# First dense layer of a fused attention and MLP kernel: two 128x512 tiles in two neighbouring PSUM banks, one tanh and one product for both

## The chip, the cores and the metric

The kernel runs on one core of one Trainium2 chip. The metric is the device time of one execution in microseconds; the time before is the median of three runs. Line numbers (L623) are those of the kernel before, as the profile uses them. Engines: PE is TensorE, ACT ScalarE, DVE VectorE, POOL GpSimd, SP the engine that issues most DMAs.

## The reference

```python
def _A_ref(x, wq, wk, wv, wo):              # 32 heads of 16, one shared key and value head
    q = (x @ wq).reshape(B, S, H, Dh).transpose(0, 2, 1, 3)
    k = x @ wk
    v = x @ wv
    p = softmax(einsum("bhqd,bkd->bhqk", q, k) * Dh ** -0.5)
    o = einsum("bhqk,bkd->bhqd", p, v)
    return o.transpose(0, 2, 1, 3).reshape(B, S, H * Dh) @ wo

def _B_ref(x, w1, w2):
    return einsum("bsf,fd->bsd", silu(einsum("bsd,df->bsf", x, w1)), w2)

xn = layernorm(x)                            # x: 1 x 2048 x 512, F = 1792, all bf16
return x + _A_ref(xn, wq, wk, wv, wo) * silu(_B_ref(xn, w1, w2))
```

## The kernel before

**What is computed in which tiles.** Queries come in 4 chunks of 512 (c), heads in 8 groups of 4 (g), so there are 32 groups (gi); keys come in 16 tiles of 128 (kt). For one group and one key tile there are four score blocks of 128 keys x 512 queries, one per head; they use four row quarters of the TensorE array. 32 x 16 x 4 = 2048 blocks have to be exponentiated. A *tile* of attention is the four blocks of one group and key tile, and the planner gives each tile to one of two engines:

- ScalarE: two blocks go into the two banks of psA0 or psA1 (`fill_A`), and one ACTIVATE of 1024 columns exponentiates both into `pa_sb` (`exp_A`, L623).
- VectorE: each block goes into a single bank out of D, D1 (the two halves of psD) and F (psF) (`fill_D`), and one TENSOR_SCALAR (`exp_D`, L661) turns it into an int16 whose bits are a rough exponential. Two blocks in D and D1 may go in one instruction of 1024 columns. When all four blocks of a tile are done, POOL makes two shifted copies (`shift`, L686), and the three together weigh out the error.

The products with the values (`emit_PV`, L745) run in four column quarters into psO, one group of four matmuls for a ScalarE block of each head, three for a VectorE block.

**Dense work.** The first layer of the MLP is the jobs `("h", c, ft)`: 4 chunks x 14 tiles of 128 rows of F, each of 4 groups of 4 column matmuls ("slots") into bank F. Silu is made as (tanh(z/2) + 1) * z: when the matmuls are done ScalarE makes a tanh of the bank into `t_sb` (`emit_tanh`, L1061), and VectorE multiplies it with the bank into `u_sb` (`evac`, L1093). The factors of a half are taken up later. The second layer is the jobs `("z", tt)`, 16 of 14 slots each, with the same tanh and product into `tmp_sb`. Jobs `q` (queries of a chunk, 4 slots), `w` and `wp` (output projection, 4 and 3 slots) use bank F as well, and end with one VectorE instruction.

PSUM has eight banks here: psA0 and psA1 two each, psD two, psO one, psF one.

**What sets the order.** The order of every engine's instructions is written out ahead by a planner in the kernel's Python: it keeps a clock per engine with its own costs, and semaphores are put where the order needs them. Its loop goes round once for each ScalarE exponential: it takes some slots of other TensorE work (a dense job if the dense work is behind its plan, else PV), and then `score_run` puts one burst of score matmuls: the two ScalarE blocks, and in the same burst, on the other row quarters, VectorE blocks for the banks that are free (`fill_D`). A burst may start when psA is free again (`release`) and is wanted 0.685 us before ScalarE's end (`needed`); a bank that becomes free up to SLIP = 0.2 us after the burst's start is still taken. `fill_D` is called from the burst alone while ScalarE has tiles left. A tanh is put in front of the next exponential when its bank is ready (`tanh_ready`). `hold` says whether a bank has a VectorE block ("blk") or a dense job ("job"); bank F goes to a dense job if one is due. VectorE's instructions are taken as they become ready (`advance_v`).

How many tiles go to VectorE isn't fixed: `next_D` opens another tile whenever a free bank asks for a block, and ScalarE goes on with what is left.

The lines that carry this in `score_run` are

```python
            fill_A(tile, rows, state["n"] % 2)
            fill_D(t, other(rows))
            if tanh_ready(K.act_end - TGATE):
                emit_tanh()
            exp_A(tile[0], [(i, tile[1], None, 512 * m) for m, i in enumerate(rows)])
```

Of the kernel before, what the change touches and what calls it, by code (L numbers as in the profile page):

```python
# [5 lines left out]
ACT = mybir.ActivationFunctionType  # L6
# [7 lines left out]
P = 128  # L14
# [201 lines left out]
def bass_recurrent_scan__grouped_kv_mqa__dense_activation_silu__prompt_kernel(  # L216
# [24 lines left out]
    NPA = 11  # L241
    DEFER, PATIENCE = .2,8
    NPD = 4
    NPS = 3
    NGN = 2
    NOB = 4
# [26 lines left out]
    with ExitStack() as es:  # L273
        def sb(name, shape, dt=BF16):
            return es.enter_context(nc.sbuf_tensor(name, shape, dt))
# [114 lines left out]
        def stats_act(t):  # L390

            r = D ** -0.5
            op("a", lambda e: e.activation(scr_sb[:, 1:2], eps_sb[:, 0:1], ACT.Sqrt), reads=["eps"], writes=["scr1"], cost=4)
            op("a", lambda e: e.activation(t_sb[:, 0, :], x_sb[:, t, :], ACT.Copy, scale=1.0 / D, accum_out=mv_sb[:, t, 0:1]),
               reads=[("x", t)], writes=[("t", 0), ("mean", t)], cost=NQ)
            op("a", lambda e: e.activation(nm_sb[:, 0:1], mv_sb[:, t, 0:1], ACT.Copy, scale=r), reads=[("mean", t)],
               writes=["nm"], cost=4)
            op("a", lambda e: e.activation(t_sb[:, 1, :], x_sb[:, t, :], ACT.Square, scale=-r, bias=nm_sb[:, 0:1],
                                           accum_out=mv_sb[:, t, 1:2]),
               reads=[("x", t), "nm"], writes=[("t", 1), ("mv", t)], cost=NQ)  # L400

# [470 lines left out]

        dense = [("h", 0, ft) for ft in range(NFT)]
        for c in range(1, NC):
            for ft in range(NFT):
                dense.append(("h", c, ft))
                if ft in (2, 6, 9, 13):
                    dense.append(("z", 4 * (c - 1) + (2, 6, 9, 13).index(ft)))  # L880
# [96 lines left out]
        def next_job(t):  # L977
# [3 lines left out]
                return None  # L981
            return next((jb for jb in jobs[:AHEAD] if startable(jb, t)), None)

        def job_ready(t):
            if jst["open"]:
                return True
            return bool(jobs and "F" in free_banks(t + 0.04) and next_job(t))

        def emit_job(t, n):
            if not jst["open"]:  # L990
                jb = next_job(t)
                jobs.remove(jb)
                b = "F"
                jst.update(open=jb, part=0, bank=b)
                hold[b] = "job"
            jb, b = jst["open"], jst["bank"]
            k, ap = jb[0], bank_ap(b)
            items = list(range(jst["part"], min(SIZE[k], jst["part"] + n)))
            end = SIZE[k] - 1
            if k in ("h", "q"):  # L1000
                _, c, ft = jb
                w, name = (w1_sb, "w1") if k == "h" else (wq_sb, "wq")
                rd = xnT_keys(c) + [name]

                def pair(m):
                    return w[:, m, ft * P:(ft + 1) * P], xnT_sb[:, m, c * NQ:(c + 1) * NQ]
# [19 lines left out]
            op("pe", f, reads=rd, writes=[b], cost=("col", [0, 1, 2, 3] * len(items), NQ))  # L1026
            jst["part"] += len(items)
            if k != "wp":
                jst["slots"] += len(items)
            if jst["part"] == SIZE[k]:  # L1030
                jst["open"] = None
                if k in ("h", "z"):
                    jst["tanh"].append((jb, b))
                else:
                    task(k, evac, 0.69, jb=jb, bank=b, reads=[b], writes=[])
                if k in ("z", "w"):
                    tok.add((k + "mm", jb[1]))
            return len(items)
# [13 lines left out]

        def tanh_ready(t):
            return jst["tanh"] and (state["nt"] < 2 or ("tev", state["nt"] - 2) in tok) and \
                K.ready("a", [jst["tanh"][0][1]], [("t", state["nt"] % 2)]) <= t

        def emit_tanh():
            jb, b = jst["tanh"].pop(0)
            n = state["nt"]
            state["nt"] += 1  # L1060
            op("a", lambda e: e.activation(t_sb[:, n % 2, :], bank_ap(b), ACT.Tanh, scale=0.5 if jb[0] == "h" else 0.25),  # L1061
               reads=[b], writes=[("t", n % 2)], cost=NQ)
            task(jb[0], evac, 0.685, jb=jb, bank=b, n=n, reads=[b, ("t", n % 2)], writes=[])

        def load_xr(tt):
            if tt < NT:
# [10 lines left out]

        def add(tk):
            tt = tk["jb"][1]
            final_add("v", tt, fin_sb[:, tt % 2, :], ("fin", tt % 2))  # L1080
            tok.add(("add", tt))

        def evac(tk):
            k, jb, b = tk["kind"], tk["jb"], tk["bank"]
            src = bank_ap(b)
            hold[b] = None
            if k in ("h", "z"):
                n = tk["n"]
                if k == "h":
                    dst, key = u_sb[:, jb[1] % 2, jb[2], :], ("u", jb[1] % 2, jb[2])  # L1090
                else:
                    dst, key = tmp_sb[:, (jb[1] // 4) % 2, jb[1] % 4, :], ("tmp", jb[1] % 8)
                op("v", lambda e: e.scalar_tensor_tensor(out=dst, in0=t_sb[:, n % 2, :], scalar=1.0, in1=src,  # L1093
                                                         op0=ALU.add, op1=ALU.mult),
                   reads=tk["reads"], writes=[key], cost=tk["cost"])
                tok.add(("tev", n))
                tok.add((k + "ev",) + jb[1:])
            elif k == "q":
                _, c, t = jb
                op("v", lambda e: e.tensor_scalar(qT_sb[:, c % 2, t, :], src, QSCALE, None, op0=ALU.mult),  # L1100
# [1 line left out]
                tok.add(jb)  # L1102
            elif k == "w":
                tt = jb[1]
                op("v", lambda e: e.scalar_tensor_tensor(out=fin_sb[:, tt % 2, :], in0=src, scalar=0.25,
                                                         in1=tmp_sb[:, (tt // 4) % 2, tt % 4, :],
                                                         op0=ALU.mult, op1=ALU.mult),
                   reads=[b, ("tmp", tt % 8)], writes=[("fin", tt % 2)], cost=tk["cost"])
                tok.add(("wev", tt))
                task("add", add, 0.42, jb=jb, reads=[("fin", tt % 2), ("x", 12 + tt % 4)], writes=[])  # L1110
# [165 lines left out]
        def extra_fill():  # L1276
# [6 lines left out]
            ride = max(needed(), t + 0.2) + 0.43  # L1283
            best = None
            for b in BANKS:
                if hold[b] is None and (b != "F" or not jobs or not behind(F_BEHIND) or not next_job(t)):
# [221 lines left out]
```

## Time and profile before

| | |
|---|---|
| Median of three runs | 676.16 us (676.15 to 676.19) |
| Profiled execution | 676.35 us, of which the span of the trace is 674.5 |
| Mean granted TensorE clock | 0.998 |
| ScalarE busy | 666.4 us (99%), 769 instructions: 677 exponentials, 72 tanhs and a few others |
| TensorE busy | 651.8 us (97%) |
| VectorE busy | 586.9 us (87%), 986 instructions |
| POOL busy | 364.3 us (54%), 371 instructions |
| First-layer tiles | 56 tanhs and 56 products of 128x512 |

Busy time is the union of the instructions' durations. Instructions of an engine overlap in this profile (one starts before the last has ended), so the spacing of two starts or ends, and not the duration, is what an instruction costs an engine that is always busy. The number behind a bar in the rows of groups is the engine's idle time just ahead of the group, with what ended it.

### The profile page before, as it was taken

What the parts mean: (1) busy time and instruction counts of PE and PEld (TensorE: products, weight loads), DVE (VectorE), ACT (ScalarE), POOL (GpSimd) and SP (SyncE); (2) the same over time, 40 slices, a digit from 0 to 9 for tenths busy, and PEclk for the clock granted to TensorE, in tenths of its full rate; (3) what the DMA queues carried; (4) which work ended last, traced back from release to release, by engine and by line L of the source; (5) the groups of instructions that cost most, each with busy time, mean ns of one, the idle gap of its engine ahead of it and who ended that gap; (6) DMA issues with size and microseconds to landing.
All of it is one profiled execution on the core that took longest, in us unless ns stands there. A gap on an engine that the chain in (4) does not pass through costs nothing.

```text
span 674.5 us, 18636 instructions
## 1 busy us (share of the span) xinstructions
PE 651.8 (97%) x8175; PEld 184.7 (27%) x8182; DVE 586.9 (87%) x986; ACT 666.4 (99%) x769; POOL 364.3 (54%) x371
## 2 busy tenths in 40 slices
PE   8999999999999999999999999999999999999997
PEld 4422222222222222222222222222222222222221
DVE  7998889889899888988898988888898788878996
ACT  8999999999999999999999999999999999999997
POOL 3255555556556555555555655464565466645662
PEclk9999999999999999999999999999999999999999
DMA  6440000000000000000000000010000000000110
GB/s 167 148 143 2 1 2 1 2 2 1 2 2 1 17 17 18 18 1 2 2 1 3 2 1 2 2 32 29 6 2 2 1 2 2 1 2 2 32 34 32
DMA packets 12321, 12.50 MB, mean 19 GB/s; under 512 B 2512, under 2 KB 11728, under 8 KB 12240
## 3 DMA queue, kind: packets, MB, share of 16 engines
q1 hardware_dynamic: 11680, 10.78, 5.2%
q8 instruction: 64, 1.05, 0.7%
q10 hardware_dynamic: 560, 0.52, 0.2%
q14 instruction: 17, 0.14, 0.1%
HBM read 8.95 MB, written 2.10 MB: 16 GB/s over the span
## 4 chain that ended last, share of the span: by engine, by line
ACT 87%; PE 9%; DVE 2%; DMA 1%; SPq 1%; issue 0%
ACT pa_sb L623 82%; ACT t_sb L1061 5%; PE psA L593 3%; PE psO L745 3%; PE psF L372 2%; DMA x_sb<-in_A_x_dram 1%; PE psD L432 0%; PE psD L463 0%; DVE stats_sb L388 0%; DMA kTb_sb<-kTa_sb 0%; SPq L481 0%; DVE kTa_sb L475 0%; PE psA L639 0%; PE psD L593 0%; DVE wq_sb L1441 0%
## 5 line engine op out<-in xcount | busy, mean ns | idle before, releaser
L623 ACT ACTIVATE pa_sb<-psA 128x1024 bf16<-128x1024 f32 x677 | 642.7, 1202 | 0.9 <-PE psA L593 0.6
L686 POOL INT64_ADD ph_sb<-ph_sb x286 | 294.2, 1041 | 224.0 <-DVE ph_sb L661 224.0
L661 DVE TENSOR_SCALAR ph_sb<-psD 128x512 int16<-128x512 f32 (+1 forms) x501 | 343.2, 698 | 47.2 <-PE psD L593 39.2
L745 PE MATMUL psO<-ph_sb,vaug_sb 128*32 128x512 bf16 x1716 | 216.2, 383 | 0.2
L745 PE MATMUL psO<-pa_sb,vaug_sb 128*32 128x512 bf16 x1362 | 204.7, 383 | 0.3 <-ACT pa_sb L623 0.3
L593 PE MATMUL psA<-qT_sb,kTa_sb 32*128 32x512 bf16 x692 | 134.2, 384 | 7.9 <-ACT pa_sb L623 6.3
L593 PE MATMUL psA<-qT_sb,kTb_sb 32*128 32x512 bf16 x654 | 126.8, 384 | 7.5 <-ACT pa_sb L623 6.7
L593 PE MATMUL psD<-qT_sb,kTb_sb 32*128 32x512 bf16 x328 | 117.7, 384 | 0.2 <-DMA kTb_sb<-kTa_sb 0.2
L593 PE MATMUL psD<-qT_sb,kTa_sb 32*128 32x512 bf16 x301 | 106.8, 384 | 0.0
L661 DVE TENSOR_SCALAR x_sb<-psD 128x512 int16<-128x512 f32 (+1 forms) x111 | 76.3, 694 | 15.6 <-PE psD L593 14.5
L686 POOL INT64_ADD x_sb<-x_sb x60 | 61.7, 1041 | 51.5 <-DVE x_sb L661 51.5
L593 PEld LDWEIGHTS psA<-qT_sb,kTa_sb 32*128 32x128 bf16 x692 | 32.5, 90 | 147.2 <-ACT pa_sb L623 135.1
L593 PEld LDWEIGHTS psA<-qT_sb,kTb_sb 32*128 32x128 bf16 x654 | 30.7, 91 | 143.6 <-ACT pa_sb L623 134.7
L372 PE MATMUL psF<-xnT_sb,w_sb 128*32 128x512 bf16 x896 | 69.5, 384 | 0.0
L372 PE MATMUL psF<-w_sb,u_sb 128*32 128x512 bf16 x896 | 69.0, 384 | 0.0
L745 PE MATMUL psO<-x_sb,vaug_sb 128*32 128x512 bf16 x366 | 68.0, 384 | 0.0
L745 PEld LDWEIGHTS psO<-ph_sb,vaug_sb 128*32 128x32 bf16 x1716 | 53.2, 94 | 48.0 <-issue 31.2
L745 PEld LDWEIGHTS psO<-pa_sb,vaug_sb 128*32 128x32 bf16 x1362 | 50.7, 94 | 46.6 <-issue 33.6
L1061 ACT ACTIVATE t_sb<-psF 128x512 bf16<-128x512 f32 x72 | 55.7, 774 | 0.0
L1093 DVE SCALAR_TENSOR_TENSOR u_sb<-t_sb,psF 128x512 bf16<-128x512 bf16 x56 | 38.2, 683 | 11.0 <-ACT t_sb L1061 8.8
L661 DVE TENSOR_SCALAR ph_sb<-psF 128x512 int16<-128x512 f32 x56 | 38.1, 680 | 0.0
L593 PEld LDWEIGHTS psD<-qT_sb,kTb_sb 32*128 32x128 bf16 x328 | 28.1, 91 | 0.6 <-DMA kTb_sb<-kTa_sb 0.5
(131 smaller groups left out, 362.1 us busy)
## 6 DMA issues: line engine op xcount, KB each, us to landing
w_sb<-in_B_w_dram SPq DMA_DIRECT2D x2, 1792.0 KB, 8.6
x_sb<-in_A_x_dram SPq DMA_DIRECT2D x18, 128.0 KB, 2.3
out_dram<-ob_sb SPq DMA_DIRECT2D x14, 128.0 KB, 1.7
x_sb<-in_A_x_dram SPq DMA_DIRECT2D x3, 512.0 KB, 5.7
wop_sb<-in_A_wo_dram SPq DMA_DIRECT2D x1, 512.0 KB, 4.0
wq_sb<-in_A_wq_dram SPq DMA_DIRECT2D x1, 384.0 KB, 6.5
x_sb<-in_A_x_dram ACTq DMA_DIRECT2D x2, 128.0 KB, 2.9
kTb_sb<-kTa_sb SPq DMA_DIRECT2D x16, 16.0 KB, 2.6
```

Source lines behind the costliest of these rows:

```text
L372: r = e.matmul(bank[32 * i:32 * i + 32, :], lhsT=lhsT[:, 32 * i:32 * i + 32], rhs=rhs, start=start, stop=stop, tile_position=(0, 32 * i), ...
L593: return e.matmul(ap, lhsT=kT_sb[g % 2][32 * i:32 * i + 32, kt * P:(kt + 1) * P], rhs=qT_sb[32 * i:32 * i + 32, c % 2, g // 2, :], start=T ...
L623: d = op("a", lambda e: e.activation(pa_sb[:, sl, :], psA[k][:, :], ACT.Exp, scale=ESCALE), reads=["A%d" % k], writes=[("pa", sl)], cost=2 ...
L661: d = op("v", lambda e: e.tensor_scalar(ph_ap(0, sl, 512 * pos, 512 * pos + m), src, float(PH_ONE + PH_BIAS), 0.0, op0=ALU.add, op1=ALU.ma ...
L686: d = op("gp", lambda e, j=j: e.int64_add(ph_ap(j, sl, 0, 4 * NQ).bitcast(I64), ph_ap(0, sl, 0, 4 * NQ).bitcast(I64), PH_SHIFT[j] * 0x0001 ...
L745: r = e.matmul(psO[32 * i:32 * i + 32, cs], lhsT=vaug_sb[:, p["v"], p["kt"], :], rhs=p["ap"], start=s0, stop=s1, tile_position=(0, 32 * i) ...
L1061: op("a", lambda e: e.activation(t_sb[:, n % 2, :], bank_ap(b), ACT.Tanh, scale=0.5 if jb[0] == "h" else 0.25), reads=[b], writes=[("t", n ...
L1093: op("v", lambda e: e.scalar_tensor_tensor(out=dst, in0=t_sb[:, n % 2, :], scalar=1.0, in1=src, op0=ALU.add, op1=ALU.mult), reads=tk["read ...
```

## The change

First-layer jobs come in pairs: `("h", c, ft)` with even ft stands for the tiles ft and ft + 1, and has 8 slots. Slots 0 to 3 go into bank F with the weights of tile ft + 1, slots 4 to 7 into bank D1 with those of tile ft. So that both can be read in one access, psD grows to 1536 columns and psF becomes its last 512: D, D1 and F are neighbours. One tanh of 1024 columns reads D1 and F, and one product of 1024 columns writes both tiles of `u_sb`; `t_sb` has two rows of 1024. The second-layer jobs, q, w and wp stay in bank F alone, with a tanh of 512 columns.

Bank D1 is taken by the job when its second half starts, and only when it is free (`job_ready`, `emit_job`); from slot 4 on, `fill_D` keeps D1 from VectorE blocks for it. Both banks are given back when the product is put into VectorE's order. Second-layer jobs stand behind the first-layer tiles 2, 6, 8 and 12 instead of 2, 6, 9 and 13. `fin_sb` goes: the gated product of the last layer is written to `ob_sb`, and the residual is added in place.

```diff
-        t_sb = sb("t_sb", [P, 2, NQ])
+        t_sb = sb("t_sb", [P, 2, 2, NQ])
-        fin_sb = sb("fin_sb", [P, 2, D])
...
-        psD = es.enter_context(nc.psum_tensor("psD", [P, 1024], FP32))
+        psD = es.enter_context(nc.psum_tensor("psD", [P, 1536], FP32))
-        psF = es.enter_context(nc.psum_tensor("psF", [P, 512], FP32))
+        psF = psD[:, 1024:1536]
...
-        dense = [("h", 0, ft) for ft in range(NFT)]
+        dense = [("h", 0, ft) for ft in range(0, NFT, 2)]
...
-        SIZE = dict(h=4, z=NFT, q=4, w=4, wp=3)
+        SIZE = dict(h=8, z=NFT, q=4, w=4, wp=3)
...
         def job_ready(t):
             if jst["open"]:
-                return True
+                return jst["open"][0] != "h" or jst["part"] < 4 or hold["D1"] == "job" or "D1" in free_banks(t + 0.04)
...
         def emit_job(t, n):
...
+            if k == "h" and jst["part"] + n > 4 and hold["D1"] != "job":
+                if "D1" in free_banks(t + 0.04 + 0.21 * max(0, 4 - jst["part"])):
+                    hold["D1"] = "job"
+                else:
+                    n = 4 - jst["part"]
...
                 for m in items:
                     l, r = pair(m)
-                    h = columns(e, ap, l, r, m == 0, m == end)
+                    if k == "h":
+                        h = columns(e, bank_ap(("F", "D1")[m // 4]), l, r, m % 4 == 0, m % 4 == 3)
+                    else:
+                        h = columns(e, ap, l, r, m == 0, m == end)
...
         def emit_tanh():
...
-            op("a", lambda e: e.activation(t_sb[:, n % 2, :], bank_ap(b), ACT.Tanh, scale=0.5 if jb[0] == "h" else 0.25),
-               reads=[b], writes=[("t", n % 2)], cost=NQ)
+            if jb[0] == "h":
+                op("a", lambda e: e.activation(t_sb[:, n % 2, :, :].rearrange("p a n -> p (a n)"), psD[:, NQ:3 * NQ], ACT.Tanh, scale=0.5),
+                   reads=bs, writes=[("t", n % 2)], cost=2 * NQ)
+            else:
+                op("a", lambda e: e.activation(t_sb[:, n % 2, 0, :], psF[:, :], ACT.Tanh, scale=0.25),
+                   reads=bs, writes=[("t", n % 2)], cost=NQ)
...
         def evac(tk):
...
                 if k == "h":
-                    dst, key = u_sb[:, jb[1] % 2, jb[2], :], ("u", jb[1] % 2, jb[2])
+                    _, c, ft = jb
+                    dst, keys = u_sb[:, c % 2, ft:ft + 2, :], [("u", c % 2, ft), ("u", c % 2, ft + 1)]
+                    dst, tin = dst.rearrange("p a n -> p (a n)"), t_sb[:, n % 2, :, :].rearrange("p a n -> p (a n)")
+                    src2 = psD[:, NQ:3 * NQ]
...
-                op("v", lambda e: e.scalar_tensor_tensor(out=fin_sb[:, tt % 2, :], in0=src, scalar=0.25,
+                op("v", lambda e: e.scalar_tensor_tensor(out=ob_sb[:, tt % NOB, :], in0=src, scalar=0.25,
...
         def fill_D(t, free, only=None):
 
-            banks = sorted(free_banks(t + SLIP), key=lambda b: (b == "F", K.ready("pe", [], [b])))
+            jb = next_job(t) if jobs and behind(F_BEHIND) else None
+            want = ["F"]
+            if jst["open"] and jst["open"][0] == "h" and jst["part"] >= D1_PART and hold["D1"] != "job":
+                want = ["D1"]
+            banks = sorted(free_banks(t + SLIP), key=lambda b: (b in want, b == "F", K.ready("pe", [], [b])))
             if only:
                 banks = only
             keep = 0
-            if not only and "F" in banks and jobs and behind(F_BEHIND) and next_job(t):
-                keep = 1
+            if not only and (want == ["D1"] or jb and not jst["open"]):
+                keep = len(set(banks) & set(want))
```

More of the change, by code (lines that the diff above doesn't have):

```diff
@@ L243, in bass_recurrent_scan__grouped_kv_mqa__dense_activation_silu__prompt_kernel @@
     NPD = 4
+    D1_PART = 4
     NPS = 3
@@ L393, in stats_act @@
             op("a", lambda e: e.activation(scr_sb[:, 1:2], eps_sb[:, 0:1], ACT.Sqrt), reads=["eps"], writes=["scr1"], cost=4)
-            op("a", lambda e: e.activation(t_sb[:, 0, :], x_sb[:, t, :], ACT.Copy, scale=1.0 / D, accum_out=mv_sb[:, t, 0:1]),
+            op("a", lambda e: e.activation(t_sb[:, 0, 0, :], x_sb[:, t, :], ACT.Copy, scale=1.0 / D, accum_out=mv_sb[:, t, 0:1]),
                reads=[("x", t)], writes=[("t", 0), ("mean", t)], cost=NQ)
@@ L397, in stats_act @@
                writes=["nm"], cost=4)
-            op("a", lambda e: e.activation(t_sb[:, 1, :], x_sb[:, t, :], ACT.Square, scale=-r, bias=nm_sb[:, 0:1],
+            op("a", lambda e: e.activation(t_sb[:, 1, 0, :], x_sb[:, t, :], ACT.Square, scale=-r, bias=nm_sb[:, 0:1],
                                            accum_out=mv_sb[:, t, 1:2]),
@@ L871, in partial @@
                reads=["ident", ("spart", k)], writes=[key, *more], cost=("full", [None], NQ))
-        dense = [("h", 0, ft) for ft in range(NFT)]
+        dense = [("h", 0, ft) for ft in range(0, NFT, 2)]
         for c in range(1, NC):
-            for ft in range(NFT):
+            for ft in range(0, NFT, 2):
                 dense.append(("h", c, ft))
-                if ft in (2, 6, 9, 13):
-                    dense.append(("z", 4 * (c - 1) + (2, 6, 9, 13).index(ft)))
+                if ft in (2, 6, 8, 12):
+                    dense.append(("z", 4 * (c - 1) + (2, 6, 8, 12).index(ft)))
         dense += [("z", tt) for tt in range(4 * (NC - 1), 4 * NC)]
-        SIZE = dict(h=4, z=NFT, q=4, w=4, wp=3)
+        SIZE = dict(h=8, z=NFT, q=4, w=4, wp=3)
         total = sum(SIZE[jb[0]] for jb in dense) + 28 * SIZE["q"]
@@ L982, in next_job, with job_banks @@
             return next((jb for jb in jobs[:AHEAD] if startable(jb, t)), None)
+        def job_banks(jb):
+            return ["D1", "F"] if jb[0] == "h" else ["F"]
         def job_ready(t):
             if jst["open"]:
-                return True
+                return jst["open"][0] != "h" or jst["part"] < 4 or hold["D1"] == "job" or "D1" in free_banks(t + 0.04)
             return bool(jobs and "F" in free_banks(t + 0.04) and next_job(t))
@@ L992, in emit_job @@
                 jobs.remove(jb)
[L993 to L996, printed above, removed]
+                jst.update(open=jb, part=0)
+                hold["F"] = "job"
+            jb, b = jst["open"], "F"
             k, ap = jb[0], bank_ap(b)
+            if k == "h" and jst["part"] + n > 4 and hold["D1"] != "job":
[3 more added lines that the diff above has]
+                    n = 4 - jst["part"]
+            wr = [b]
             items = list(range(jst["part"], min(SIZE[k], jst["part"] + n)))
@@ L1005, in pair @@
                 def pair(m):
-                    return w[:, m, ft * P:(ft + 1) * P], xnT_sb[:, m, c * NQ:(c + 1) * NQ]
+                    f, m = (ft + 1 - m // 4 if k == "h" else ft), m % 4
+                    return w[:, m, f * P:(f + 1) * P], xnT_sb[:, m, c * NQ:(c + 1) * NQ]
+                if k == "h":
+                    wr = sorted({"FD"[m // 4] + "1" * (m // 4) for m in items})
             elif k == "z":
@@ L1023, in f @@
                     l, r = pair(m)
-                    h = columns(e, ap, l, r, m == 0, m == end)
+                    if k == "h":
+                        h = columns(e, bank_ap(("F", "D1")[m // 4]), l, r, m % 4 == 0, m % 4 == 3)
+                    else:
+                        h = columns(e, ap, l, r, m == 0, m == end)
                 return h
-            op("pe", f, reads=rd, writes=[b], cost=("col", [0, 1, 2, 3] * len(items), NQ))
+            op("pe", f, reads=rd, writes=wr, cost=("col", [0, 1, 2, 3] * len(items), NQ))
             jst["part"] += len(items)
@@ L1032, in emit_job @@
                 if k in ("h", "z"):
-                    jst["tanh"].append((jb, b))
+                    jst["tanh"].append((jb, job_banks(jb)))
                 else:
-                    task(k, evac, 0.69, jb=jb, bank=b, reads=[b], writes=[])
+                    task(k, evac, 0.69, jb=jb, bank=b, reads=[b], writes=[("ob", jb[1] % NOB)] if k == "w" else [])
                 if k in ("z", "w"):
@@ L1054, in tanh_ready @@
             return jst["tanh"] and (state["nt"] < 2 or ("tev", state["nt"] - 2) in tok) and \
-                K.ready("a", [jst["tanh"][0][1]], [("t", state["nt"] % 2)]) <= t
+                K.ready("a", jst["tanh"][0][1], [("t", state["nt"] % 2)]) <= t
         def emit_tanh():
-            jb, b = jst["tanh"].pop(0)
+            jb, bs = jst["tanh"].pop(0)
             n = state["nt"]
             state["nt"] += 1
-            op("a", lambda e: e.activation(t_sb[:, n % 2, :], bank_ap(b), ACT.Tanh, scale=0.5 if jb[0] == "h" else 0.25),
-               reads=[b], writes=[("t", n % 2)], cost=NQ)
-            task(jb[0], evac, 0.685, jb=jb, bank=b, n=n, reads=[b, ("t", n % 2)], writes=[])
+            if jb[0] == "h":
[4 more added lines that the diff above has]
+                   reads=bs, writes=[("t", n % 2)], cost=NQ)
+            task(jb[0], evac, 1.219 if jb[0] == "h" else 0.685, jb=jb, bank=bs, n=n, reads=bs + [("t", n % 2)], writes=[])
         def load_xr(tt):
@@ L1079, in add @@
             tt = tk["jb"][1]
-            final_add("v", tt, fin_sb[:, tt % 2, :], ("fin", tt % 2))
+            final_add("v", tt, ob_sb[:, tt % NOB, :], ("ob", tt % NOB))
             tok.add(("add", tt))
@@ L1084, in evac @@
             k, jb, b = tk["kind"], tk["jb"], tk["bank"]
-            src = bank_ap(b)
-            hold[b] = None
+            bs = b if isinstance(b, list) else [b]
+            src = bank_ap(bs[-1])
+            for b1 in bs:
+                hold[b1] = None
             if k in ("h", "z"):
                 n = tk["n"]
+                tin, src2 = t_sb[:, n % 2, 0, :], src
                 if k == "h":
-                    dst, key = u_sb[:, jb[1] % 2, jb[2], :], ("u", jb[1] % 2, jb[2])
-                else:
-                    dst, key = tmp_sb[:, (jb[1] // 4) % 2, jb[1] % 4, :], ("tmp", jb[1] % 8)
-                op("v", lambda e: e.scalar_tensor_tensor(out=dst, in0=t_sb[:, n % 2, :], scalar=1.0, in1=src,
+                    _, c, ft = jb
+                    dst, keys = u_sb[:, c % 2, ft:ft + 2, :], [("u", c % 2, ft), ("u", c % 2, ft + 1)]
+                    dst, tin = dst.rearrange("p a n -> p (a n)"), t_sb[:, n % 2, :, :].rearrange("p a n -> p (a n)")
+                    src2 = psD[:, NQ:3 * NQ]
+                    for f in (ft, ft + 1):
+                        tok.add(("hev", c, f))
+                else:
+                    dst, keys = tmp_sb[:, (jb[1] // 4) % 2, jb[1] % 4, :], [("tmp", jb[1] % 8)]
+                op("v", lambda e: e.scalar_tensor_tensor(out=dst, in0=tin, scalar=1.0, in1=src2,
                                                          op0=ALU.add, op1=ALU.mult),
-                   reads=tk["reads"], writes=[key], cost=tk["cost"])
+                   reads=tk["reads"], writes=keys, cost=tk["cost"])
                 tok.add(("tev", n))
-                tok.add((k + "ev",) + jb[1:])
+                if k == "z":
+                    tok.add(("zev", jb[1]))
             elif k == "q":
@@ L1104, in evac @@
                 tt = jb[1]
-                op("v", lambda e: e.scalar_tensor_tensor(out=fin_sb[:, tt % 2, :], in0=src, scalar=0.25,
+                op("v", lambda e: e.scalar_tensor_tensor(out=ob_sb[:, tt % NOB, :], in0=src, scalar=0.25,
                                                          in1=tmp_sb[:, (tt // 4) % 2, tt % 4, :],
                                                          op0=ALU.mult, op1=ALU.mult),
-                   reads=[b, ("tmp", tt % 8)], writes=[("fin", tt % 2)], cost=tk["cost"])
+                   reads=[b, ("tmp", tt % 8)], writes=[("ob", tt % NOB)], cost=tk["cost"])
                 tok.add(("wev", tt))
-                task("add", add, 0.42, jb=jb, reads=[("fin", tt % 2), ("x", 12 + tt % 4)], writes=[])
+                task("add", add, 0.42, jb=jb, reads=[("ob", tt % NOB), ("x", 12 + tt % 4)], writes=[])
             elif k == "wp":
@@ L1285, in extra_fill @@
             for b in BANKS:
-                if hold[b] is None and (b != "F" or not jobs or not behind(F_BEHIND) or not next_job(t)):
+                if hold[b] is None and (not jobs or not behind(F_BEHIND) or not next_job(t) or b != "F"):
                     r = max(t, K.ready("pe", [], [b]))
```

## The prediction, made before the changed kernel was run

> **What bounds the kernel now.** I read the page first, then the groups of instructions with shapes kept apart, the chain in order of time, the waits, the timeline of one dense tile, and last a table of stretches for the VectorE eviction alone. The page:
>
> ```profile
> PE 651.8 (97%) x8175; PEld 184.7 (27%) x8182; DVE 586.9 (87%) x986; ACT 666.4 (99%) x769; POOL 364.3 (54%) x371
> ACT 87%; PE 9%; DVE 2%; DMA 1%; SPq 1%; issue 0%
> L623 ACT ACTIVATE pa_sb<-psA 128x1024 bf16<-128x1024 f32 x677 | 642.7, 1202 | 0.9 <-PE psA L593 0.6
> L1061 ACT ACTIVATE t_sb<-psF 128x512 bf16<-128x512 f32 x72 | 55.7, 774 | 0.0
> ```
>
> ScalarE never stops: its 677 exponentials idle 0.9 us in all, its 72 tanhs not at all. The time is the number of ScalarE instructions times their spacing. The chain in order of time gives the spacing, and its shares by line give the tanh's:
>
> ```profile
> by line: ACT pa_sb L623 81.7%; ACT t_sb L1061 5.2%; PE psA L593 3.1%; PE psO L745 2.8%; PE psF L372 1.6%; DMA x_sb<-in_A_x_dram 0.9%; PE psD L432 0.4%; PE psD L463 0.4%; DVE stats_sb L388 0.4%; DMA kTb_sb<-kTa_sb 0.3%; SPq L481 0.3%; DVE kT
> 90.71 11.00 ACT pa_sb L623 x12
> ```
>
> 12 exponentials in 11.00 us: 0.917 us each. The tanhs: 5.2% of 674.5 is 35.1 us, over 72 is 0.487 us. The durations of 1202 and 774 ns overlap and are not the price.
>
> How many exponentials there are is the planner's choice: a score block (128x512) goes to ScalarE, two per exponential, or to VectorE, one per eviction on line 661 (then POOL). VectorE evictions by shape:
>
> ```profile
> L661 DVE TENSOR_SCALAR ph_sb<-psD 128x512 int16<-128x512 f32 x486 | 324.9, 682 | 43.8 <-PE psD L593 36.0 <-PE psF L593 1.8 <-PE psO L745 0.5
> L661 DVE TENSOR_SCALAR ph_sb<-psD 128x1024 int16<-128x1024 f32 x15 | 18.3, 1218 | 3.4 <-PE psD L593 3.3
> L1093 DVE SCALAR_TENSOR_TENSOR u_sb<-t_sb,psF 128x512 bf16<-128x512 bf16 x56 | 38.2, 683 | 11.0 <-ACT t_sb L1061 8.8
> ```
>
> With the other forms (x_sb 109 and 2 wide, psF 56 and 9) VectorE takes 486+30+109+4+56+9 = 694 blocks, 1.03 per exponential. It is no full engine: 13% idle, and what ends most of its waits is TensorE filling psD. Why so late is in the timeline around one dense tile:
>
> ```profile
> 164.53 0.09 PEld L593 LDWEIGHTS psA<-qT_sb,kTb_sb 32*128 32x128 bf16 x2 [0.42 <-ACT pa_sb L623]
> 164.54 0.39 PE L593 MATMUL psD<-qT_sb,kTb_sb 32*128 32x512 bf16 x1
> 165.00 0.69 DVE L661 TENSOR_SCALAR ph_sb<-psD 128x512 int16<-128x512 f32 x1 [0.16 <-PE psD L593]
> 165.02 0.75 ACT L1061 ACTIVATE t_sb<-psF 128x512 bf16<-128x512 f32 x1
> 165.80 0.69 DVE L1093 SCALAR_TENSOR_TENSOR u_sb<-t_sb,psF 128x512 bf16<-128x512 bf16 x1
> 165.85 0.38 PE L593 MATMUL psD<-qT_sb,kTb_sb 32*128 32x512 bf16 x1
> 166.75 0.39 PE L593 MATMUL psD<-qT_sb,kTb_sb 32*128 32x512 bf16 x1
> ```
>
> A VectorE block is filled only in a burst of score matmuls, and there is one burst per exponential. The bank filled at 164.54 is empty at 165.69, 1.15 us later; bursts are 0.90 to 0.92 us apart (1.30 across a tanh). A bank so misses the next burst: two banks (D, D1) give one block per burst, the third (F) some more where no dense tile holds it. Stretches packed with first-layer tiles (first two rows) against stretches with F free, line 661 alone (x counts evictions):
>
> ```profile
> 48.30:73.50 25.20, 16.65 (x26) 1.00 0.01 2
> 158.90:174.90 16.00, 10.38 (x17) 1.00 0.01 2
> 150.90:158.90 8.00, 7.37 (x12) 1.00 0.00 0
> 187.90:194.60 6.70, 6.08 (x10) 1.00 0.01 4
> ```
>
> 1.03 and 1.06 evictions per us with two banks, 1.5 with three: 0.95 to 0.97 and 1.37 per burst of 0.917 us. Counted over all 56 first-layer tiles it is 1.01 per burst.
>
> **The change, part by part.** The profiled execution took 676.35 us (span 674.5, 1.85 around it), 0.19 over the median of 676.16; differences are added to the median.
>
> *ScalarE.* 56 tanhs of 512 columns become 28 of 1024. The nearest row for the new shape is the exponential on the same tile shape, 0.917 us, against 2 x 0.487 = 0.974: 0.057 x 28 = **-1.6 us**, all on the path. Its ends are 0 (if spacing were by columns alone) and 28 x 0.063 = 1.8 (the tanh at 0.490, its spacing where exponentials stand on both sides). The Trainium skill ("ScalarE: Activation LUTs", What ACT_TABLE_LOAD costs) gives an instruction with immediate scale and bias 186 ns beside its columns, of which 93 overlap the next; by it the gain would be an estimated 2.6 us, by the rows 1.6, and the rows decide.
>
> *VectorE product.* Line 1093 at 512 columns takes 683 ns, and the next instruction starts 0.60 after it did (51.08 and 51.68 in the timeline); the 1024-column eviction on line 661 takes 1218, so a wide product holds VectorE about 1.13. Two narrow ones 1.20: 0.07 x 28 = 2 us, worth up to 3 blocks, nothing at least.
>
> *TensorE.* The 224 matmul groups of the first layer are the same. New is a wait: the second four groups need D1 empty. Behind it in TensorE's order stand PV groups and the next score burst, and behind that ScalarE. The planner starts them only when it reckons D1 free; a miss hides in the 0.42 us that TensorE waits for ScalarE before a burst (269.7 us, 609 times). Cost 0, and without that cover each miss would be a ScalarE gap of its own length, some 0.2 us: at worst 28 x 0.2 = 5.6 us, which I don't expect.
>
> *Banks, the part that decides.* A narrow tile holds F for 3.58 us (162.91 to 166.49: matmuls 1.48, wait for its turn 0.63, tanh 0.75, product 0.69); all 56 average 3.65. A pair: matmuls of the first tile 1.83 (two exponentials), of the second 1.48, wait 0.5, tanh 1.2, product 1.22: F for 6.2 us, D1 for the last **4.4 us**. In those, VectorE's blocks have one bank. Bursts in them: (4.4 - 0.92 for the tanh) / 0.917 = 3.8 per pair, 106 in all.
> - One bank's rate has no row. Bounds: one block in two bursts (turnaround 1.15 over spacing 0.917: it misses every second) and one per burst, as now. The planner can put a burst up to 0.18 us late without delaying ScalarE (it wants a burst 0.685 us ahead of ScalarE's end, and may start 0.917 - 0.05 ahead) and takes a bank that is 0.2 late (SLIP), so a refill after 0.917 + 0.38 = 1.30 us can just be made once, and then not again: two in three. I take 0.67: 106 x (1.01 - 0.67) = 36 blocks lost; ends 0 and 106 x 0.51 = 54.
> - D1 is kept empty ahead of the second half: half a burst per pair at half a block, 7 lost; ends 0 and 14.
> - F comes back earlier: 2 x 3.65 - 6.2 = 1.1 us per pair, 1.2 bursts x 28 = 34 at 1.37 - 1.01: 12 gained; at the mean over all stretches with F free (1.14 per burst) 4.
> - The product: 3 gained; ends 0 and 3.
>
> Net 36 + 7 - 12 - 3 = 28 blocks. They go where all others do: each added exponential takes 2, and its burst feeds VectorE 1.1 more. 28 / 3.1 = 9 exponentials x 0.917 = **+8.3 us**; with the tanhs **+6.7**. Ends: 54 + 14 - 4 = 64 blocks, 20.6 x 0.917 - 1.6 = +17.3; and 0 - 15, -4.8 x 0.917 - 1.6 = -6.0.
>
> One section of the Trainium skill ("Perfetto Trace Analysis", Optimizing Scalar/DVE Operations) points both ways: group into larger operations where the engine is saturated, break up where ScalarE or VectorE isn't saturated but makes others wait. Here ScalarE (99%) falls under the first and VectorE (87%) under the second; its per-instruction 51 ns for ScalarE on PSUM would be an estimated 1.4 us gained, and the second rule has no price.
>
> *The rest.* The gated product of the last layer writes ob_sb, and its add works in place: same shapes, same count, and the store of four tiles before (1.7 us to landing in the page) has long landed. The order of second-layer tiles shifts by one first-layer tile: 0. SP's queue gets the same transfers. Planner choices shift everywhere, and one VectorE tile more or fewer is 2 exponentials, 1.8 us either way.
>
> **Rivals.**
> 1. *Faster: one bank suffices.* The wide tanh parts two bursts by 1.83 us, the wide product covers VectorE for 1.13, and bursts slide so that D is refilled nearly each time. Break-even: 1.6 us is 1.75 exponentials, 5.4 blocks; with 7 lost and 15 gained elsewhere, one bank must give 1.01 - 13.4/106 = 0.88 per burst. Above it -1 to -6 us, likeliest -2.5: 673.7. For: VectorE is 86% busy in the first packed stretch (21.63 of 25.2 us), so little more is to be had there anyway. Against: 1.15 > 0.917.
> 2. *Every second burst, and D1 late:* 54 + 14 - 7 = 61 blocks, 19.7 x 0.917 - 1.6 = +16: 692. For: bank and spacing as measured, with no luck. Against: the slack of 0.38 us, and the longer gap across a tanh (1.30 held a refill).
> 3. *Nothing to measure:* loss and gain cancel at some 5 blocks, within 1.35 us (0.2%, about what a measurement of this kernel can tell from no change): 676.
>
> **How the numbers follow.** Forecast (two in three, +2 to +12): 0.61. Rival 2 (+12 to +17): 0.13. Rival 3: 0.07. Rival 1: 0.19. So slower 0.74, same 0.07, faster 0.19. Predicted 676.2 + 6.7 = 682.9 us. The forecast's own range is 678 to 688; the one given reaches down to the likeliest of rival 1 and up into rival 2: 673.5 to 691, which leaves out about 0.1 at each end.
>
> **What would show it.** In the profile after: 28 rows of a 128x1024 tanh with 0.917 to the next exponential (-1.6 confirmed); 28 products near 1.22; exponentials up from 677 to some 686 and blocks on line 661 down from 694 to some 676 (POOL's adds from 346 to some 337); ScalarE's idle still about 1 us; VectorE's idle for "PE psD" up from 53.7 us, inside the stretches in which D1 belongs to a pair. Exponentials at 677 or fewer mean that one bank was enough, and I am wrong; 695 or more, rival 2. ScalarE idle of some us would mean that the new wait in TensorE's queue reached the path.

## The result, and the profile after

The changed kernel takes 691.61 us (median of 4, 690.89 to 692.18) where the kernel before takes 676.15 beside it: a ratio of 1.0229, 95% interval 1.0211 to 1.0247. That is 15.5 us slower; the prediction said slower, by 6.7 us, and its range ended at 691.0. The page of the profile after:

```profile
PE 663.7 (96%) x8158; PEld 188.1 (27%) x8165; DVE 561.5 (81%) x930; ACT 681.1 (99%) x759; POOL 346.0 (50%) x353
L623 ACT ACTIVATE pa_sb<-psA 128x1024 bf16<-128x1024 f32 x695 | 651.2, 1198 | 2.0 <-PE psA L593 1.3
L1120 DVE SCALAR_TENSOR_TENSOR u_sb<-t_sb,psD 128x1024 bf16<-128x1024 bf16 x28 | 34.1, 1219 | 22.5 <-ACT t_sb L1077 22.5
L1077 ACT ACTIVATE t_sb<-psD 128x1024 bf16<-128x1024 f32 x28 | 33.7, 1205 | 0.0
```

ScalarE is as full as before and has 18 exponentials more (695 for 677). VectorE went from 87% to 81%, POOL from 364 to 346 us: work moved from them to the engine that sets the time. 18 x 0.917 = 16.5 us; 1.6 less for the wide tanhs; 1.1 more idle ahead of the exponentials (0.9 before, 2.0 now): 16.0, beside a span that grew by 15.8. The chain in order of time has the wide tanh at its price, as one piece of 0.92 us:

```profile
69.65 0.92 ACT t_sb L1077
```

The waits show where VectorE's share went, again to TensorE filling psD: 53.7 us before (the first two lines), 87.5 now (the last two). Bank F counts as psD now; its 2.3 us of before would make it 56.0.

```profile
DVE ph_sb L661 <- PE psD L593: 39.2, 137, 1.1
DVE x_sb L661 <- PE psD L593: 14.5, 46, 2.8
DVE ph_sb L661 <- PE psD L593: 65.6, 160, 3.7
DVE x_sb L661 <- PE psD L593: 21.9, 51, 1.4
```

The wide product also waits longer for its tanh, 22.5 us for 8.8 before. Whether the wide instructions themselves cost anything, an experiment below tells.

And this is one pair in the timeline, from the first matmul in D1 to the end of the product (weight loads, PV and some other lines left out):

```profile
167.80 0.62 PE L372 MATMUL psD<-xnT_sb,w_sb 128*32 128x512 bf16 x8
168.35 0.39 PE L593 MATMUL psA<-qT_sb,kTb_sb 32*128 32x512 bf16 x2
168.36 0.39 PE L593 MATMUL psD<-qT_sb,kTb_sb 32*128 32x512 bf16 x1
168.72 0.42 DVE L833 TENSOR_TENSOR onb_sb<-otr_sb,rcp_sb 128x256 bf16<-128x256 f32 x1
169.06 0.68 DVE L661 TENSOR_SCALAR ph_sb<-psD 128x512 int16<-128x512 f32 x1
169.22 0.39 PE L593 MATMUL psA<-qT_sb,kTb_sb 32*128 32x512 bf16 x2
169.77 1.21 ACT L1077 ACTIVATE t_sb<-psD 128x1024 bf16<-128x1024 f32 x1
170.52 0.39 PE L593 MATMUL psA<-qT_sb,kTb_sb 32*128 32x512 bf16 x2
170.53 0.39 PE L593 MATMUL psD<-qT_sb,kTb_sb 32*128 32x512 bf16 x1
171.01 1.22 DVE L1120 SCALAR_TENSOR_TENSOR u_sb<-t_sb,psD 128x1024 bf16<-128x1024 bf16 x1 [1.27 <-ACT t_sb L1077]
171.95 0.39 PE L593 MATMUL psA<-qT_sb,kTb_sb 32*128 32x512 bf16 x2
172.15 0.68 DVE L661 TENSOR_SCALAR ph_sb<-psD 128x512 int16<-128x512 f32 x1
```

Each psA line is a burst. Those at 168.35 and 170.52 carry a block for VectorE (the psD line beside them), those at 169.22 and 171.95 carry none: the bank filled at 168.36 is emptied at 169.74 and filled again at 170.53. Here VectorE is busy when the bank is ready, first with line 833, then with the product; in most pairs it isn't, and the bank is empty 1.15 us after the fill began. Either way, in none of the 28 pairs do two bursts in a row carry a block. The table of stretches, cut to the time in which D1 belongs to a pair and to line 661, has two or three evictions in each of the 28, for 4 or 5 bursts (three of its rows, and the sum):

```profile
67.44:71.83 4.39, 1.39 (x2) 1.00 0.01 2
167.80:172.23 4.43, 0.76 (x2) 1.00 0.00 0
240.56:245.63 5.07, 1.38 (x2) 1.00 0.06 20
sum 129.66, DVE 35.69; mean DVE 1.27
```

Counting score matmuls into VectorE's banks, and bursts, in the trace:

| stretch | bursts | blocks filled | per burst |
|---|---|---|---|
| before: a first-layer tile holds F | 177 | 178 | 1.01 |
| after: the pair holds F and D1 | 117 | 56 | **0.48** |
| after: the pair holds F alone | 64 | 55 | 0.86 |
| before, 45 to 625 us, no such tile | 417 | 452 | 1.08 |
| after, 45 to 625 us, no pair | 414 | 475 | 1.15 |

### The profile page after: what moved, and what is told of

The parts are those of the page before. It is cut to its first block, busy times and chain, and to the rows that moved or that the text cites. A ratio compares the mean times of both kernels' runs of the same rounds, so it can differ in the third digit from the quotient of the medians.

```text
span 690.3 us, 18510 instructions
## 1 busy us (share of the span) xinstructions
PE 663.7 (96%) x8158; PEld 188.1 (27%) x8165; DVE 561.5 (81%) x930; ACT 681.1 (99%) x759; POOL 346.0 (50%) x353
## 4 chain that ended last, share of the span: by engine, by line
ACT 85%; PE 10%; DVE 2%; DMA 1%; SPq 0%; issue 0%
ACT pa_sb L623 81%; PE psA L593 4%; ACT t_sb L1077 4%; PE psO L745 3%; PE psD L372 2%; ACT t_sb L1080 1%; DMA x_sb<-in_A_x_dram 1%; PE psD L432 0%; PE psD L463 0%; DVE ph_sb L661 0%; DVE stats_sb L388 0%; DMA kTb_sb<-kTa_sb 0%; SPq L481 0%; PE psD L379 0%; PE psO L372 0%
## 5 line engine op out<-in xcount | busy, mean ns | idle before, releaser
L623 ACT ACTIVATE pa_sb<-psA 128x1024 bf16<-128x1024 f32 x695 | 651.2, 1198 | 2.0 <-PE psA L593 1.3
L686 POOL INT64_ADD ph_sb<-ph_sb x266 | 274.0, 1042 | 258.5 <-DVE ph_sb L661 258.4
L661 DVE TENSOR_SCALAR ph_sb<-psD 128x512 int16<-128x512 f32 x526 | 346.8, 690 | 68.8 <-PE psD L593 65.6
L745 PE MATMUL psO<-pa_sb,vaug_sb 128*32 128x512 bf16 (+1 forms) x1398 | 202.4, 383 | 0.6 <-DVE onb_sb L857 0.6
L593 PE MATMUL psD<-qT_sb,kTb_sb 32*128 32x512 bf16 x334 | 109.7, 386 | 0.2 <-DMA kTb_sb<-kTa_sb 0.2
L372 PE MATMUL psD<-xnT_sb,w_sb 128*32 128x512 bf16 x896 | 70.1, 384 | 0.0
L372 PE MATMUL psD<-w_sb,u_sb 128*32 128x512 bf16 x896 | 69.1, 384 | 0.0
L1120 DVE SCALAR_TENSOR_TENSOR u_sb<-t_sb,psD 128x1024 bf16<-128x1024 bf16 x28 | 34.1, 1219 | 22.5 <-ACT t_sb L1077 22.5
L1077 ACT ACTIVATE t_sb<-psD 128x1024 bf16<-128x1024 f32 x28 | 33.7, 1205 | 0.0
L593 PEld LDWEIGHTS psD<-qT_sb,kTa_sb 32*128 32x128 bf16 x324 | 25.7, 91 | 0.3
```

Of the source, the lines that this page charges most:

```text
L372: r = e.matmul(bank[32 * i:32 * i + 32, :], lhsT=lhsT[:, 32 * i:32 * i + 32], rhs=rhs, start=start, stop=stop, tile_position=(0, 32 * i), ...
L593: return e.matmul(ap, lhsT=kT_sb[g % 2][32 * i:32 * i + 32, kt * P:(kt + 1) * P], rhs=qT_sb[32 * i:32 * i + 32, c % 2, g // 2, :], start=T ...
L623: d = op("a", lambda e: e.activation(pa_sb[:, sl, :], psA[k][:, :], ACT.Exp, scale=ESCALE), reads=["A%d" % k], writes=[("pa", sl)], cost=2 ...
L661: d = op("v", lambda e: e.tensor_scalar(ph_ap(0, sl, 512 * pos, 512 * pos + m), src, float(PH_ONE + PH_BIAS), 0.0, op0=ALU.add, op1=ALU.ma ...
L686: d = op("gp", lambda e, j=j: e.int64_add(ph_ap(j, sl, 0, 4 * NQ).bitcast(I64), ph_ap(0, sl, 0, 4 * NQ).bitcast(I64), PH_SHIFT[j] * 0x0001 ...
L745: r = e.matmul(psO[32 * i:32 * i + 32, cs], lhsT=vaug_sb[:, p["v"], p["kt"], :], rhs=p["ap"], start=s0, stop=s1, tile_position=(0, 32 * i) ...
```

## The experiments

Times are medians; the kernel before took 676.1 to 676.3 us beside them.

**Is it the bank or the wide instructions?** `f_alone` keeps the wide tanh and product and gives the bank back.

> The changed kernel without bank D1: both tiles of a pair are made in F, the second four matmul groups over the first, and the tanh and the product of 1024 columns read F twice. Left out: the first of the two tiles that is made, whose place gets the other's values. Same matmuls, same 28 wide tanhs and products, same order rules, D1 never taken. Bank theory (the loss is the 117 bursts in which VectorE's blocks had one bank): exponentials back to 677, plus or minus 3 by the planner's luck, 676.2 - 1.6 = 674.6 us, range 671 to 678. Wide-instruction theory (the product of 1.22 us and its wait for a tanh of 1.2 hold VectorE up): about the changed kernel's 691.6.

```diff
...
-    psD[:, NQ:3 * NQ], ACT.Tanh                      # D1 and F
+    psF[:, :].unsqueeze(1).to_broadcast([P, 2, NQ]), ACT.Tanh
-    h = columns(e, bank_ap(("F", "D1")[m // 4]), l, r, m % 4 == 0, m % 4 == 3)
+    h = columns(e, bank_ap("F"), l, r, m % 4 == 0, m % 4 == 3)
...
```

The second, `rest_only`, has all of the change but the pairs.

> The kernel before with all of the change but the pairs: ob_sb in place of fin_sb, psF as the end of psD, second-layer jobs behind the same pairs (tiles 3, 7, 9, 13). Bank theory: 677 exponentials plus or minus 3, 676.2 us plus or minus 3. Theory that the order of jobs or the planner's luck made the loss: up to 690 exponentials and 690 us.

```diff
...
-                if ft in (2, 6, 9, 13):
+                if ft in (3, 7, 9, 13):
...
-                op("v", lambda e: e.scalar_tensor_tensor(out=fin_sb[:, tt % 2, :], in0=src, scalar=0.25,
+                op("v", lambda e: e.scalar_tensor_tensor(out=ob_sb[:, tt % NOB, :], in0=src, scalar=0.25,
```

`f_alone` took 676.12 us (ratio 1.0002, 0.9992 to 1.0012), `rest_only` 677.82 (1.0026, 1.0016 to 1.0036); both have 679 exponentials. So the wide instructions cost no exponentials; taking D1 makes 679 into 695. The rest of the change costs 2 exponentials, 1.7 us. And since the two differ in the wide instructions and the pairing, with as many exponentials, 1.7 us is what these gain: the -1.6 of the prediction. In `f_alone` 0.99 blocks go into a burst while a pair holds F. VectorE still waits there for TensorE's fills, 69.1 us, and for the tanh, 10.6: waits of that size cost no exponentials as long as a bank is there for the blocks.

**The price of the bank by itself.**

> The kernel before, tiles single and narrow; D1 stands empty, kept from VectorE's blocks, while an odd first-layer tile holds F, where D1 is free when the tile starts (16 of 28). Bank theory: 16 x (3.65 - 0.49) / 0.917 = 55 bursts with one bank x (1.01 - 0.48) = 29 blocks, 29 / 3.1 = 9 exponentials, +8.6 us: 684.8 (681 to 689). Wide-instruction theory: there is none here, 676.2.

```diff
                 hold[b] = "job"
+                if jb[0] == "h" and jb[2] % 2 and hold["D1"] is None:
+                    hold["D1"] = "job"
...
```

689.06 us (1.0193, 1.0177 to 1.0208), just above the 689 that was the most expected, and 691 exponentials: with the old instructions, and D1 idle beside 16 of 56 tiles, most of the loss is there. In the tiles 160 blocks went into 189 bursts, 31 fewer than at 1.01, where 29 were expected. But they cost 14 exponentials and not 9, since the loss is not in the tiles alone. Outside them, over the whole span, 506 blocks went into 502 bursts, where the kernel before has 516 in 500: 12 fewer at the same rate. Together 43 blocks; each added exponential takes 2 and its burst 1.03, so 43 / 3.03 = 14. With 2048 blocks in all this sum must close; what the trace adds is where they were lost. The prediction's way of dividing holds, and what the expectation left out is the 12 blocks outside. Why the rate falls there is not shown. It makes idle D1 dearer here than in the changed kernel: 14 exponentials for some 51 us (16 x 3.2) of it, there 16 for 130 us.

> The changed kernel with D1 taken together with F at a pair's start, 2.1 us earlier. Bank theory: the 64 bursts of the changed kernel in which the pair held F alone go from 0.86 to 0.48 blocks, 24 blocks, 8 exponentials, +7.2 us over the changed kernel: 699 (695 to 703). Wide-instruction theory: 691.6, nothing wide is added or moved.

```diff
                 hold["F"] = "job"
+                if jb[0] == "h":
+                    hold["D1"] = "job"
```

702.93 us (1.0400, 1.0384 to 1.0415), 708 exponentials, 11.3 us over the changed kernel: a longer hold costs more. The stretch before the second half fell to 0.46 blocks per burst, as expected (48 bursts instead of 64). Outside the pairs the rate was lower too, 1.10 where the changed kernel has 1.15, which the estimate of 7.2 left out.

**Undoing the wide instructions, and a shorter hold.** Two experiments that did not go as the simple account has it.

> The changed kernel with two tanhs and two products of 512 columns for a pair, both banks held until the second product. Wide-instruction theory: back to some 678 us. Bank theory: as the changed kernel or worse, tanhs +1.6 us, D1 and F held about as long: 692 to 697.

701.18 us (1.0373, 1.0357 to 1.0388), 700 exponentials: going back to narrow instructions with the banks held saves nothing, and the wide-instruction theory falls a second time. The size was missed. Both tanhs of my kernel carry the same key, so the planner lets the second wait for the first. In the trace the ends of a tanh pair lie 0.490 and 0.629 us after the one before, 1.12 for 0.917 wide: 28 x 0.20 = 5.7 us, and 5 exponentials are 4.6. D1 is held longer with them, 4.95 us for 4.63, and the rate outside is 1.11 for 1.15; how the 5 exponentials divide between these is not shown. The timeline shows the two and the next exponential 1.25 us after their start:

```profile
62.31 1.35 ACT L1078 ACTIVATE t_sb<-psD 128x512 bf16<-128x512 f32 x2
63.56 6.52 ACT L623 ACTIVATE pa_sb<-psA 128x1024 bf16<-128x1024 f32 x7
```

> The changed kernel with two products of 512 columns after the wide tanh; D1 is given back after the first, 0.6 us earlier than F. If the loss were simply bursts with D1 away times 0.53 blocks, 28 x 0.6 / 0.917 = 18 bursts fewer, 10 blocks, 3 exponentials: 689. Against it the planner lays out 700 exponentials for this kernel, 5 more than the changed one's 695, which would be 696: then the time of the hold is not all that counts, and the trace tells where the blocks are lost (in the pair or after it).

695.07 us (1.0277, 1.0264 to 1.0291), 700 exponentials. The hold of D1 did shrink, to 95 bursts with 44 blocks; 52 are lost there instead of 62. But the pair now keeps F 7.3 us instead of 6.7, the stretch with F alone grew to 77 bursts at 0.79, and the rate outside fell from 1.15 to 1.10, for a reason that is not shown. D1's hold is the largest item but not the only one.

**Why one block in two bursts?** Two candidates: the turnaround of the bank, and the planner's `hold`, which counts a bank as free only when its eviction stands in VectorE's order. That order is brought up to date at the head of the loop, before the burst's time, when the eviction of a block just filled isn't ready yet. The trace of the changed kernel already speaks for the second: after 39 fills there is another burst in the pair; in 18 cases the bank had been emptied before that burst began (the burst came 1.30 to 1.51 us after the fill, the end of the eviction 1.15 to 1.33), and that burst filled it in none of the 18. A two by two:

> The changed kernel; while D1 belongs to a pair the planner puts evictions that are ready by the burst into VectorE's order before it chooses banks for the burst, so that a bank filled in the burst before can count as free. Turnaround theory (a bank is full for 1.15 us, bursts are 0.917 apart): nothing changes, 0.48 blocks per burst, 691.6 us. Bookkeeping theory (the bank is empty in time now and then, but still counted as full): two in three, 117 x 0.19 = 22 blocks, 7 exponentials fewer, 685.

```diff
             t = max(t, release())
+            if hold["D1"] == "job":
+                advance_v(t + 0)
...
```

> The changed kernel; while D1 belongs to a pair an eviction takes 128 of the 512 columns (the rest of those blocks is left out). Turnaround falls to about 0.46 + 0.3 = 0.8 us, under the spacing of 0.917. Turnaround theory: one block per burst, 117 x 0.53 = 62 blocks, 18 exponentials fewer, about 675. Bookkeeping theory: the bank still counts as full at the next burst, 0.48 stays, 691 less some VectorE time, 688 to 692.

```diff
+            if hold["D1"] == "job" and len(blks) == 1:
+                q, cost = 128, 0.287
...
-            d = op("v", lambda e: e.tensor_scalar(ph_ap(0, sl, 512 * pos, 512 * pos + m), src,
+            d = op("v", lambda e: e.tensor_scalar(ph_ap(0, sl, 512 * pos, 512 * pos + q), src[:, 0:q],
...
```

> Both edits together: evictions of 128 columns while D1 belongs to a pair (the rest of those blocks left out) and the evictions put in order ahead of the choice of banks. If each of the two holds the bank by itself, only this one gets to near one block per burst: up to 62 blocks, exponentials down to 677 to 685, 675 to 683 us. If turnaround alone counts, the same as with short evictions alone; if bookkeeping alone, the same as with the order edit alone.

| | turnaround as it is | evictions of 128 columns |
|---|---|---|
| order as it is | changed kernel: 0.48 per burst, 695 exponentials, 691.61 us | `short_evict`: 0.48, 692, 689.02 (1.0190, 1.0175 to 1.0205) |
| evictions ordered first | `look`: 0.56, 695, 692.37 (1.0239, 1.0222 to 1.0256) | `look_short`: **0.97**, 684, 680.74 (1.0067, 1.0052 to 1.0082) |

Neither alone brings the rate much above a half; both together double it, and 11 of the 18 exponentials come back. A bank here is held by two locks. Most of the other seven lie in the stretch in which the pair holds F alone, where `look_short` has 48 blocks in 62 bursts, 14 fewer than at 1.01.

`look` also shows what the turnaround lock is. After a fill the next burst of the pair refilled the bank in none of the 31 cases in which it came up to 1.30 us later, and in all 11 in which it came 1.35 us later or more. In 13 of the 31 the gap was 1.30 us and the bank had been empty since 1.15 or 1.16. So the planner wants more time than the chip takes. One reason can be read in its code: it asks for banks that are free by its time at the head of the loop, or by `release` if that is later, plus SLIP, and other TensorE work is put between that time and the burst. No run changes this, so its share is not shown.

The timeline of `look_short` (its lines stand three further down) has one block in every burst of the pair that begins at 105.60, where the changed kernel has one in two (one line of another instruction left out):

```profile
105.30 0.29 DVE L664 TENSOR_SCALAR ph_sb<-psD 128x128 int16<-128x128 f32 x1 [0.30 <-PE psD L593]
106.39 0.29 DVE L664 TENSOR_SCALAR ph_sb<-psD 128x128 int16<-128x128 f32 x1 [0.18 <-PE psD L593]
107.26 0.29 DVE L664 TENSOR_SCALAR ph_sb<-psD 128x128 int16<-128x128 f32 x1 [0.58 <-PE psD L593]
108.13 0.29 DVE L664 TENSOR_SCALAR ph_sb<-psD 128x128 int16<-128x128 f32 x1 [0.58 <-PE psD L593]
109.43 0.29 DVE L664 TENSOR_SCALAR ph_sb<-psD 128x128 int16<-128x128 f32 x1 [1.01 <-PE psD L593]
109.64 1.21 DVE L1123 SCALAR_TENSOR_TENSOR u_sb<-t_sb,psD 128x1024 bf16<-128x1024 bf16 x1
```

**A faster kernel?** If missed bursts keep blocks off VectorE in the kernel before as well, later bursts should help it.

> The kernel before, single narrow tiles, with bursts of scores allowed 0.1 us later (wanted 0.585 us ahead of ScalarE's end, not 0.685). If a bank that misses a burst is what keeps blocks off VectorE here too, a later burst finds more banks free: 675 exponentials for 677, -1.8 us, 674.4, if ScalarE doesn't wait. If TensorE then comes late, ScalarE idles and the gain is lost: 676 or more.

> The kernel before with bursts allowed 0.15 us later, no filler matmuls (KEEP 0) and dense work let fall 8 slots less behind (F_BEHIND 8). The planner lays out 670 exponentials, 7 fewer: -6.4 us, 669.8, if ScalarE never waits for a burst; for each 0.1 us that it waits at a tenth of them the gain shrinks by 6.7 us, so that a time above 676 means bursts that come late.

Both are rule values of the planner alone (MARGIN, and KEEP and F_BEHIND in the second). 676.11 us (0.9997, 0.9988 to 1.0006) with 675 exponentials, and 685.67 (1.0132, 1.0108 to 1.0155) with 670. The bursts do find more banks, and ScalarE then waits: in the second its idle ahead of the exponentials is 8.0 us for 0.9 and the mean granted TensorE clock 0.988 for 0.998, and the ends of neighbouring exponentials are 0.945 us apart on average, for 0.918 before and 0.921 in the first. How much of that is the lower clock is not shown; the fastest run of the second, at a clock of 1.000, still took 680.9 us. None of the versions beats the kernel before.

```profile
L623 ACT ACTIVATE pa_sb<-psA 128x1024 bf16<-128x1024 f32 x670 | 635.7, 1071 | 8.0 <-PE psD L593 3.3
```

## Why the prediction was wrong

*Direction and mechanism were right.* ScalarE stayed the bound, the wide tanh gave its 1.6 us (1.7 between `f_alone` and `rest_only`), the new wait of TensorE for D1 reached the path with about 1 us at most (ScalarE's added idle), and the loss is VectorE's blocks in the time in which D1 belongs to a pair. On the tanh the trace decides between row and page: by the figure of the Trainium skill ("ScalarE: Activation LUTs", What ACT_TABLE_LOAD costs) the gain was an estimated 2.6 us, by the rows 1.6.

*The step that failed is the rate of one bank,* "two in three. I take 0.67". Measured: 0.48, in 117 bursts instead of 106 (D1 was held 4.63 us, not 4.4). The term is 117 x (1.01 - 0.48) = 62 blocks, not 36. The prediction reasoned that bursts could slide by 0.38 us to meet a bank that turns round in 1.15. It read `SLIP` and `needed`, and not the third condition, `hold`, that keeps the bank out of the choice whatever the time; the two by two shows that condition and the turnaround, each of which is nearly enough by itself (0.48 with the first alone, 0.56 with the second). The prediction had the right number as the bound of one block in two bursts (54 blocks) and as rival 2, with a chance of 0.13 and a time of 692. No row spoke for 0.67 over 0.5, and one spoke for 0.5: its own 1.01 per burst with two banks is a block in every second burst for each.

It set against rival 2 that a gap of 1.30 us across a tanh "held a refill". The rows at 164.54 and 165.85 don't show that, because two banks were in use there. Besides the one filled at 164.54 there was one filled at 163.68 and emptied at 164.84:

```profile
163.68 0.38 PE L593 MATMUL psD<-qT_sb,kTb_sb 32*128 32x512 bf16 x1
164.21 0.63 DVE L661 TENSOR_SCALAR ph_sb<-psD 128x512 int16<-128x512 f32 x1
```

In the changed kernel none of the 25 gaps of 1.28 us and more behind a fill held one.

*The other terms.* D1 kept empty ahead: 64 x (1.01 - 0.86) = 10 blocks, 7 forecast. Gains outside the pairs: 547 blocks in 514 bursts over the whole span, where the rate of before (516 in 500) gives 530, so 17 gained; 12 and 3 were forecast. That this sum came out is luck as far as it rests on F's earlier return: `f_alone` holds F about as long (6.84 us for 6.72), and its rate outside is 1.09, the 1.08 of before. What raised it to 1.15 in the changed kernel is not shown. All together 62 + 10 - 17 = 55 blocks; over 3.03 that is the 18 exponentials. With 117 bursts and 0.48 the prediction's own sum gives 62 + 7 - 12 - 3 = 54 blocks, 17.4 exponentials, +14.4 us: one term makes nearly all of the miss.

*Planner's luck* was put at one VectorE tile, 1.8 us; `rest_only` has it at 1.7.

The Trainium skill ("Perfetto Trace Analysis", Optimization Strategy) reads a gap that repeats through a stretch, on the engine that should be saturated, as a possible sign that SBUF or PSUM has no room for the next tile. The trace agrees on the cause, since a withheld bank made the gaps, but they stand on VectorE (its idle ended by TensorE filling psD: 87.5 us for 53.7), which isn't the saturated engine; the full one, ScalarE, shows 2.0 us of them and more instructions instead.

## What to carry to other kernels

Where one engine is always full and another takes over as much as its buffers let it, a buffer's price is the work that falls back on the full engine: here 28 holds of 4.6 us of one bank in three cost 16 instructions of 0.917 us (695 for the 679 of `f_alone`), some nine times what the merged instructions saved. Before a merge that keeps two buffers until the longer instruction is done, count how often the buffer turns round against how often it can be filled, and count whole refills. If an order is planned ahead, read every condition by which the planner calls a buffer free: the turnaround is only one of them, and a faster eviction alone (`short_evict`) bought 2.6 us of 15.

## What the runs showed that I had not expected

Each bank gave about a block in every second burst, however many there were: 0.46 to 0.50 blocks per burst with one bank in five kernels, 0.56 in `look`, 1.01 with two. One bank reached 0.97 once both locks were off. A ScalarE instruction that waits for the one ahead of it on the same engine costs 0.14 us beyond its spacing (0.629 for 0.490).
